# Linear attention and a GELU layer on one core: the third input of the first batch loaded in three parts, and two of its casts given to ScalarE

## The chip, the core and the metric

The kernel runs on one core of one Trainium2 chip. The metric is device time in microseconds (us) of one execution; 283.94 us is the median of three for the kernel before. Five engines of the core appear below: TensorE does the matmuls (PE in the profile, PEld for the loading of its weights), VectorE (DVE), ScalarE (ACT) and GpSimd (POOL) work on tiles, and SyncE (SP) issues most of the transfers (DMA).

## What is computed

Cut to what matters, the reference is this:

```python
batch, n_heads, seq, head_dim = (8, 8, 576, 64)        # q, k, v: float32
def phi(x): return np.where(x > 0, x, np.exp(x) - 1.0) + 1.0
q_p, k_p = (phi(q), phi(k))
kv  = np.einsum('bhsd,bhse->bhde', k_p, v)
z   = np.sum(k_p, axis=2)
num = np.einsum('bhsd,bhde->bhse', q_p, kv)
den = np.einsum('bhsd,bhd->bhs', q_p, z)[..., None] + 1e-06
x = (num / den).transpose(0, 2, 1, 3).reshape(4608, 512)
h = x @ w_in                                            # w_in 512 x 2048
g = gelu_tanh(h)
out = g @ w_out                                         # w_out 2048 x 512, out 4608 x 512 float32
```

The kernel does the matmuls in bfloat16, so every float32 input that reaches TensorE is first cast by one of the other engines. For v that is a plain cast; for q and k it happens inside phi.

## The kernel before

The eight batches are worked through in turn, the attention part of a batch being mixed into the two large matmuls of the batch ahead of it. Only batches 0 and 1 are touched by the change, and batch 0 has nothing ahead of it to hide in.

All early loads are issued at the top, on one queue, in the order in which they are needed. Heads lie in four pairs; of one pair a partition holds 576 adjacent float32 numbers (nine positions of 64).

```python
    def load_pairs(name, src, b, us=slice(0, NP)):          # NP = 4 pairs, J = 9, D = 64
        s = src[b].rearrange("h s d -> (h s d)").rearrange("(u n f) -> n u f", n=P, f=J * D)
        nc.sync.dma_start(out=ld[name, b][:, us, :], in_=s[:, us, :])
    ...
    halves = (slice(0, 2), slice(2, 4))
    for s in range(2):
        load_q_paired(0, (s,))
        load_pairs("k", k, 0, halves[s])
    for s in range(2):
        load_pairs("v", v, 0, halves[s])
    for i in range(4):
        load_w_in(i, 2 if i == 0 else 1)
    load_w_out(0)
    ...                                                     # q of batch 1, w_out(1), k of batch 1
    load_w_out(2, slice(0, 2))
    ld_tile("v", 1)
    load_pairs("v", v, 1)
    load_w_out(2, slice(2, 4))
    load_w_out(3, slice(0, 2))
    load_w_out(3, slice(2, 4))
```

The cast of v writes into a tile whose rows are 65 wide (the 65th column is the one that gives the denominator) and in which the four pairs alternate. So it reads the numbers of a partition in one run, and writes each pair as nine strips of 64 that lie 260 elements apart:

```python
    vps = [pkv.tile([P, J * NP, E], BF16, name=f"vp{i}") for i in range(2)]     # E = 65
    def cast_v_paired(b, us, fn):
        fn(
            out=vp_paired(b)[:, :, us, 0:D].rearrange("p j u d -> p u j d"),
            in_=ld["v", b][:, us].rearrange("p u (j d) -> p u j d", d=D),
        )
```

The first batch, in the order of the program (each engine takes its own instructions in this order):

```python
        keep_warm(18)                                       # matmuls on zeros
        for s in range(2):
            for n, hs in (("q", qs[s]), ("k", halves[s])):
                exp_of(n, 0, hs)                            # ScalarE
                linear_of(n, 0, hs)                         # VectorE
                least_of(n, 0, hs)                          # VectorE
        transpose_q(0, nc.scalar.copy)                      # 8 transposes, copied out by ScalarE
        keep_warm(8)
        transpose_q(1, nc.scalar.copy)
        keep_warm(5)
        for ii in range(2):
            cast_v_paired(0, halves[ii], nc.vector.tensor_copy)
        kv_ps = [bank("kv_ps", [P, E]) for _ in range(2)]
        kv_paired(0, 0, lambda a, ii: kv_ps[a])             # 36 matmuls: pairs 0 and 1
        for a, fn in enumerate((nc.vector.tensor_copy, nc.scalar.copy)):
            kv_evac(0, slice(2 * a, 2 * a + 1), kv_ps[a].rearrange("p (i e) -> p i e", i=1), fn)
        keep_warm(1)
        kv_ps = pair_of_banks("kv_ps")
        kv_paired(0, 1, lambda a, ii: kv_ps[:, a, 0:E])     # 36 matmuls: pairs 2 and 3
        kv_evac(0, slice(1, 4, 2), kv_ps[:, :, 0:E], nc.vector.tensor_copy, nc.scalar.copy)
        ...                                                 # GpSimd casts w_in and w_out
        nab_half(x[0], qt[:, 0], 0)                         # numerators and denominators
        nab_half(x[0], qt[:, 0], 1)
        ...                                                 # then x, its transposes, the first large matmul
```

Batch 1 is prepared while batch 0 is in its large matmuls: a step named `at(0, n, ...)` is issued after slot n of these. `transpose_q` and `casts` come after slot 23, `kv` after slot 27, and slot 28 is the first matmul that needs rows 10 and 11 of w_out:

```python
        def transpose_q():
            qts[b] = pt.tile([P, C, NP, P], BF16, name="qt")
            for s in range(2):
                t_ps = bank("t_ps", [P, 2, NP, P], BF16)
                ...                                         # 8 transposes
                nc.scalar.copy(qts[b][:, 2 * s : 2 * s + 2], t_ps)

        def casts():
            cast_v_paired(b, slice(0, NP), nc.vector.tensor_copy)
            cast_w_out(2, nc.vector.tensor_copy, slice(2, 4))

        def kv():
            kv_ps = [bank("kv_ps", [P, 2, E]) for _ in range(2)]
            for ii in range(2):
                kv_paired(b, ii, lambda a, ii: kv_ps[a][:, ii, :])
            ...
        at(0, 15, maps)
        at(0, 23, transpose_q)
        at(0, 23, casts)
        at(0, 27, kv)
```

Of the kernel before, what the change touches and what calls it, by code (L numbers as in the profile page):

```python
# [15 lines left out]
def kernel(  # L16
# [16 lines left out]
    nc = tc.nc  # L33
# [8 lines left out]
    NP = H // 2  # L42
# [36 lines left out]
    def bank(name, shape, dt=FP32):  # L79
        return ps_b.tile(shape, dt, name=name, tag="b")  # L80

    def pair_of_banks(name):
        return ps_a.tile([P, 2, 512], FP32, name=name, tag="a")
# [9 lines left out]
    def load_pairs(name, src, b, us=slice(0, NP)):  # L93
        s = src[b].rearrange("h s d -> (h s d)").rearrange("(u n f) -> n u f", n=P, f=J * D)
        nc.sync.dma_start(out=ld[name, b][:, us, :], in_=s[:, us, :])  # L95
# [55 lines left out]
    halves = (slice(0, 2), slice(2, 4))  # L151
    for n in "qkv":
        ld_tile(n, 0)
    for s in range(2):
        load_q_paired(0, (s,))
        load_pairs("k", k, 0, halves[s])
    for s in range(2):
        load_pairs("v", v, 0, halves[s])
    for i in range(4):
        load_w_in(i, 2 if i == 0 else 1)  # L160
    load_w_out(0)
# [29 lines left out]
    def vp_paired(b):  # L191
        return vps[b % 2].rearrange("p (j u) e -> p j u e", u=NP)
# [19 lines left out]
    def exp_of(name, b, hs=None):  # L212
        x = ld[name, b]
        hs = hs or slice(0, x.shape[1])
        if (name, b) not in exps:
            e = name + ("_e" if name != "qr" or b % 2 else "_f")
            exps[name, b] = pe.tile([P, x.shape[2] // D, x.shape[1], D], BF16, name=e)
        o, i = maps_view(name, b, x, exps[name, b], hs)
        nc.scalar.activation(o, i, AF.Exp)  # L219

    def linear_of(name, b, hs=None):
        x = ld[name, b]
        hs = hs or slice(0, x.shape[1])
        if (name, b) not in phi:
            phi_tiles(name, b)
        o, i = maps_view(name, b, x, phi[name, b], hs)
        nc.vector.tensor_scalar(o, i, 1.0, 1.0, op0=ALU.add, op1=ALU.max)  # L227

    def least_of(name, b, hs=None):
        p, e = phi[name, b], exps[name, b]  # L230
        if hs:
            p, e = p[:, :, hs, :], e[:, :, hs, :]
        nc.vector.tensor_tensor(p, p, e, op=ALU.min)  # L233
# [3 lines left out]
# [5 lines that stand above are left out]
# [169 lines left out]
    def first_batch():  # L411
        w_ps = bank("w_ps", [P, 512])

        def keep_warm(n):
            for _ in range(n):
                nc.tensor.matmul(w_ps, lhsT=warm[:, 0:P], rhs=warm)  # L416

        qt = pt.tile([P, C, NP, P], BF16, name="qt")
        qs = (slice(0, 4), slice(4, 8))

        def transpose_q(s, fn):
            t_ps = bank("t_ps", [P, C, 2, P], BF16)
            for i in range(2):
                for c in range(C):
                    h = 4 * s + 2 * i
                    nc.tensor.transpose(
                        t_ps[:, c, i, :], phi["q", 0][:, c, h : h + 2, :], ident
                    )
            fn(out=qt[:, :, 2 * s : 2 * s + 2, :], in_=t_ps)

        keep_warm(18)
        for s in range(2):
            for n, hs in (("q", qs[s]), ("k", halves[s])):
                exp_of(n, 0, hs)
                linear_of(n, 0, hs)
                least_of(n, 0, hs)
        transpose_q(0, nc.scalar.copy)
        keep_warm(8)
        transpose_q(1, nc.scalar.copy)
        keep_warm(5)  # L440
        for ii in range(2):
            cast_v_paired(0, halves[ii], nc.vector.tensor_copy)
        kv_ps = [bank("kv_ps", [P, E]) for _ in range(2)]
        kv_paired(0, 0, lambda a, ii: kv_ps[a])
        for a, fn in enumerate((nc.vector.tensor_copy, nc.scalar.copy)):
# [3 lines that stand above are left out]
        kv_paired(0, 1, lambda a, ii: kv_ps[:, a, 0:E])  # L449
        kv_evac(0, slice(1, 4, 2), kv_ps[:, :, 0:E], nc.vector.tensor_copy, nc.scalar.copy)  # L450
        for fs in (slice(0, 128), slice(128, 256), slice(256, 512)):
            cast_w_in(0, nc.gpsimd.tensor_copy, fs)
        cast_w_in(1, nc.gpsimd.tensor_copy, slice(256, 512))
        for i in range(2, 4):
            cast_w_in(i, nc.gpsimd.tensor_copy)
        for i in range(2):
            cast_w_out(i, nc.gpsimd.tensor_copy)

        xts[0] = pt.tile([P, NP, MAIN], BF16, name="xt")
        x = {0: x_tile()}  # L460

        def t(c, blocks=range(NP)):
            transpose_x(x[c], xt_chunk(0, c), nc.scalar.copy, blocks)

        def h(m, c, blocks=range(KM)):
            h_begin(0, m, slice(P * c, P * (c + 1)), blocks)

        first, second = range(2), range(2, 4)
        nab_half(x[0], qt[:, 0], 0)
        nab_half(x[0], qt[:, 0], 1)  # L470
        x[1] = nab(qt[:, 1], 0)
        t(0, first)
        h_begun[0][0] = bank("h_ps", [P, MAIN])
        nc.tensor.matmul(h_begun[0][0], lhsT=warm[:, 0:P], rhs=warm, skip_group_check=True)
        t(0, second)
        for m in range(2):
            h(m, 0, first)
        x[2] = nab_in_banks(qt[:, 2], 0)
        h(0, 0, second)
        t(1)  # L480
        h(1, 0, second)
        x[3] = nab(qt[:, 3], 0)
        cast_w_in(1, nc.vector.tensor_copy, slice(0, 256))
        h(2, 0)
        h(3, 0)
        t(2)
        for m in range(3):
            h(m, 1)
        t(3)
        gelu_table()  # L490
        h(3, 1)
        for c in (2, 3):
            for m in range(4):
                h(m, c)

    first_batch()


# [12 lines left out]
    def plan_second():  # L511
        b = 1
        x = {}

        def maps():
            for n in "qk":
                exp_of(n, b)
            cast_w_out(2, nc.scalar.copy, slice(0, 2))
            for n in "qk":
                linear_of(n, b)  # L520
            for n in "qk":
                least_of(n, b)
# [5 lines that stand above are left out]
                for c in range(2):  # L528
                    for i in range(NP):
                        nc.tensor.transpose(  # L530
                            t_ps[:, c, i, :],
                            phi["q", b][:, 2 * s + c, 2 * i : 2 * i + 2, :],
                            ident,
                        )
                nc.scalar.copy(qts[b][:, 2 * s : 2 * s + 2], t_ps)

        def casts():
            cast_v_paired(b, slice(0, NP), nc.vector.tensor_copy)
            cast_w_out(2, nc.vector.tensor_copy, slice(2, 4))

        def kv():
# [4 lines that stand above are left out]
                kv_evac(b, slice(2 * a, 2 * a + 2), kv_ps[a], fn)  # L546

        def last_w_out():
            for m, fn in enumerate((nc.gpsimd.tensor_copy, nc.scalar.copy) * 2):
                cast_w_out(3, fn, slice(m, m + 1))  # L550
            gelu_table()

        def n(c):
            x[c] = (nab_in_banks if c == 1 else nab)(qts[b][:, c], b)

        def t(c):
            if c == 0:
                xts[b] = pt.tile([P, NP, MAIN], BF16, name="xt")
            transpose_x(x[c], xt_chunk(b, c), nc.scalar.copy)
# [5 lines that stand above are left out]
        at(0, 27, last_w_out)  # L565
        at(0, 29, n, 0)
        at(0, 29, n, 1)
        at(0, 32, n, 2)
        at(0, 32, t, 0)
        at(0, 33, t, 1)  # L570
        at(0, 33, n, 3)
        at(0, 34, t, 2)
        at(0, 34.5, t, 3)
        at(0, 35, h_begin, b, 0, slice(0, 3 * P))
        at(0, 35, h_begin, b, 0, slice(3 * P, MAIN))
# [253 lines left out]
```

## Time and profile before

| what | value |
|---|---|
| time, median of three | 283.94 us (283.93 to 284.04) |
| span of the profiled execution | 282.1 us |
| TensorE busy | 276.1 us, 98% of the span |
| VectorE, ScalarE, GpSimd busy | 102.6, 164.3, 15.0 us |
| granted TensorE clock | 0.998 |
| nine casts of v on VectorE | 11.0 us in all |

The span runs from the first to the last instruction. The profile gives each engine's busy time, a picture of the span in 40 slices, the chain of work that ended last (each step followed back to what released it), and the groups of instructions with their shapes. The timeline lists one engine's instructions in order: start, length, line and operation, tiles, and in brackets how long the engine had been idle and what ended that. A count such as "x2" means that neighbouring instructions of one kind are merged, the length being that of the whole stretch. Ends of matmuls are modelled, so the start of the next one is the better mark.

### The profile page before, as it was taken

To read this page: it belongs to the slowest core of one execution; us is meant where nothing else is said; L and a number is where in the kernel's file an instruction comes from. 1 tells how busy PE (TensorE), PEld (TensorE's weight loads), DVE (VectorE), ACT (ScalarE), POOL (GpSimd) and SP (SyncE) were. 2 spreads that over 40 slices of the span, in tenths; PEclk is the share of its full clock that TensorE was granted. 3 is DMA by queue.
4 is the path that set the end of the run, shared out by engine and by line. 5 is a ranking of instruction groups with operands and counts; after the bars stand their busy time and mean duration, and the time that the engine had idled before them with its cause. 6 is when DMAs were issued, how large, how long until landed. Compare 5 with 4: busy or idle time off the path is not lost.

```text
span 282.1 us, 5465 instructions
## 1 busy us (share of the span) xinstructions
PE 276.1 (98%) x2341; PEld 135.3 (48%) x2341; DVE 102.6 (36%) x177; ACT 164.3 (58%) x224; POOL 15.0 (5%) x21
## 2 busy tenths in 40 slices
PE   8899999999999999999999999999999999999995
PEld 3474455445444544454445444544444444444444
DVE  3850386344955750356034640350124001400001
ACT  4678878786986905692569346833681364026400
POOL 3147210000000000000000000000000000000000
PEclk9999999999999999999999999999999999999999
DMA  7999999978899767916794740056405300520022
GB/s 245 401 406 397 410 402 404 404 251 222 185 379 294 263 153 212 380 26 168 188 388 114 151 131 0 2 151 168 94 2 149 114 0 2 142 81 0 2 74 74
DMA packets 59591, 53.83 MB, mean 191 GB/s; under 512 B 35760, under 2 KB 45360, under 8 KB 59568
## 3 DMA queue, kind: packets, MB, share of 16 engines
q1 hardware_dynamic: 56784, 44.58, 51.0%
q10 hardware_dynamic: 2784, 8.91, 8.7%
q8 instruction: 18, 0.29, 0.4%
q14 instruction: 5, 0.04, 0.0%
HBM read 36.70 MB, written 9.44 MB: 164 GB/s over the span
## 4 chain that ended last, share of the span: by engine, by line
PE 94%; DMA 3%; SPq 1%; DVE 1%; issue 0%; ACT 0%
PE o_ps L725 44%; PE h_ps L384 44%; DMA v_x<-in_v_dram 3%; PE n_ps L322 1%; PE n_ps L249 1%; PE kv_ps L249 1%; PE n_ps L265 1%; PE t_ps L377 1%; SPq L95 1%; SPq L100 0%; PE t_ps L530 0%; DVE vp L238 0%; DVE x L367 0%; DVE kvbd L261 0%; DVE o_sb L686 0%
## 5 line engine op out<-in xcount | busy, mean ns | idle before, releaser
L725 PE MATMUL o_ps<-w_out_sb,g 128*128 128x512 bf16 (+2 forms) x608 | 128.4, 368 | 0.0
L384 PE MATMUL h_ps<-xt,w_in_sb 128*128 128x512 bf16 (+1 forms) x564 | 113.7, 359 | 0.0
L394 ACT ACTIVATE g<-h_ps 128x512 bf16<-128x512 f32 x144 | 84.5, 599 | 36.4 <-PE h_ps L384 35.1
L384 PEld LDWEIGHTS <-w_in_sb 128*128 128x128 bf16 x628 | 58.5, 98 | 64.7
L725 PEld LDWEIGHTS <-g 128*128 128x128 bf16 x608 | 57.4, 98 | 63.5
L686 ACT COPY o_sb<-o_ps 128x512 f32<-128x512 f32 (+1 forms) x19 | 10.8, 576 | 65.7 <-PE o_ps L725 58.9
L686 DVE COPY o_sb<-o_ps 128x512 f32<-128x512 f32 (+1 forms) x19 | 12.2, 645 | 50.5 <-PE o_ps L725 45.6
L282 DVE RECIPROCAL r<-n_ps 128x6 f32<-128x6 f32 (+2 forms) x43 | 8.2, 191 | 60.9 <-PE n_ps L322 55.4
L227 DVE TENSOR_SCALAR k_p<-k_x 128x2304 bf16<-128x2304 f32 (+1 forms) x9 | 11.0, 1222 | 24.4 <-DMA k_x<-in_k_dram 24.4
L283 DVE TENSOR_TENSOR xs<-n_ps,r 128x384 bf16<-128x384 f32 (+1 forms) x30 | 17.5, 584 | 1.0
L219 ACT ACTIVATE k_e<-k_x 128x2304 bf16<-128x2304 f32 (+1 forms) x9 | 17.1, 1902 | 0.9 <-DMA k_x<-in_k_dram 0.8
L219 ACT ACTIVATE q_e<-q_x 128x2048 bf16<-128x2048 f32 (+1 forms) x9 | 15.5, 1719 | 2.8 <-DMA q_x<-in_q_dram 2.7
L227 DVE TENSOR_SCALAR q_p<-q_x 128x2048 bf16<-128x2048 f32 (+1 forms) x9 | 9.9, 1102 | 13.1 <-DMA q_x<-in_q_dram 13.1
L384 PE MATMUL h_ps<-xt_rest,w_in_sb 128*128 128x512 bf16 x64 | 14.0, 379 | 0.0
L233 DVE TENSOR_TENSOR q_p<-q_p,q_e 128x2048 bf16<-128x2048 bf16 (+1 forms) x9 | 9.9, 1100 | 6.9 <-ACT q_e L219 6.8
L407 ACT ACT_TABLE_LOAD x9 | 11.5, 1283 | 0.2
L233 DVE TENSOR_TENSOR k_p<-k_p,k_e 128x2304 bf16<-128x2304 bf16 (+1 forms) x9 | 11.0, 1221 | 1.2 <-ACT k_e L219 1.0
L238 DVE CAST vp<-v_x 128x2304 bf16<-128x2304 f32 (+1 forms) x9 | 11.0, 1223 | 0.5 <-DMA v_x<-in_v_dram 0.4
L416 PE MATMUL w_ps<-warm 128*128 128x512 bf16 x32 | 9.3, 445 | 1.2 <-DVE warm L181 1.2
L219 ACT ACT_TABLE_LOAD x8 | 10.3, 1283 | 0.1
L139 POOL CAST w_in_sb<-w_st 128x512 bf16<-128x512 f32 (+2 forms) x6 | 7.6, 1271 | 14.6 <-DMA w_st<-in_moe_w_in_dram 14.6
L283 DVE TENSOR_TENSOR x<-n_ps,r 128x512 bf16<-128x512 f32 (+1 forms) x13 | 7.9, 609 | 0.4
(50 smaller groups left out, 77.5 us busy)
## 6 DMA issues: line engine op xcount, KB each, us to landing
out_dram<-o_sb ACTq DMA_DIRECT2D x16, 512.0 KB, 3.2
k_x<-in_k_dram SPq DMA_DIRECT2D x7, 1152.0 KB, 7.2
v_x<-in_v_dram SPq DMA_DIRECT2D x7, 1152.0 KB, 11.8
q_x<-in_q_dram SPq DMA_DIRECT2D x6, 1024.0 KB, 9.6
w_st<-in_moe_w_in_dram SPq DMA_DIRECT2D x3, 1024.0 KB, 13.5
q_x<-in_q_dram SPq DMA_DIRECT2D x4, 512.0 KB, 8.5
w_st<-in_moe_w_out_dram SPq DMA_DIRECT2D x2, 1024.0 KB, 12.5
w_st<-in_moe_w_out_dram SPq DMA_DIRECT2D x4, 512.0 KB, 11.2
```

The costliest lines, as they stand in the source:

```text
L219: nc.scalar.activation(o, i, AF.Exp)
L227: nc.vector.tensor_scalar(o, i, 1.0, 1.0, op0=ALU.add, op1=ALU.max)
L233: nc.vector.tensor_tensor(p, p, e, op=ALU.min)
L238: fn(out=vp_paired(b)[:, :, us, 0:D].rearrange("p j u d -> p u j d"), in_=ld["v", b][:, us].rearrange("p u (j d) -> p u j d", d=D),)
L282: nc.vector.reciprocal(r, n_v[heads + (D,)])
L283: nc.vector.tensor_tensor(x_v, n_v[heads + (slice(0, D),)], r[heads + (None,)].to_broadcast(shape + [D]), op=ALU.mult,)
L384: nc.tensor.matmul(h_ps[:, ts], lhsT=w_in_sb[:, c, P * m : P * (m + 1)], rhs=xt[:, c, ts], start=(c == 0), stop=(c == KM - 1), skip_group_ ...
L394: nc.scalar.activation(g[:, m, :], h_ps, AF.Gelu_apprx_tanh)
L407: nc.scalar.preload_act_table_set("gelu_apprx_tanh_and_others")
L416: nc.tensor.matmul(w_ps, lhsT=warm[:, 0:P], rhs=warm)
L686: (nc.scalar.copy if on_scalar else nc.vector.tensor_copy)(dst, src)
L725: nc.tensor.matmul(o_ps, lhsT=g[:, m, P * t : P * (t + 1)], rhs=w_out_sb[:, m, fs], start=(m == 0), stop=(m == MM - 1),)
```

## The change

The first batch's v comes in three loads (pairs 0 and 1 together, then pair 2, then pair 3) in place of two. Its pair 1 is cast by ScalarE between ScalarE's two copies of the transposed q; VectorE casts pairs 0, 2 and 3, one instruction each, where it had two instructions of two pairs. In batch 1 ScalarE casts pair 3 between its two copies of q, and VectorE's one cast covers three pairs where it covered four. It is meant to have v ready for its matmuls with less of the work on VectorE, and to begin the cast of a pair as soon as that pair has come.

```diff
@@ the early loads @@
-    for s in range(2):
-        load_pairs("v", v, 0, halves[s])
+    for us in (slice(0, 2), slice(2, 3), slice(3, 4)):
+        load_pairs("v", v, 0, us)
@@ first_batch @@
         transpose_q(0, nc.scalar.copy)
         keep_warm(8)
+        cast_v_paired(0, slice(1, 2), nc.scalar.copy)
         transpose_q(1, nc.scalar.copy)
         keep_warm(5)
-        for ii in range(2):
-            cast_v_paired(0, halves[ii], nc.vector.tensor_copy)
+        for u in (0, 2, 3):
+            cast_v_paired(0, slice(u, u + 1), nc.vector.tensor_copy)
@@ plan_second, batch 1 @@
                 nc.scalar.copy(qts[b][:, 2 * s : 2 * s + 2], t_ps)
+                if s == 0:
+                    cast_v_paired(b, slice(3, 4), nc.scalar.copy)
 
         def casts():
-            cast_v_paired(b, slice(0, NP), nc.vector.tensor_copy)
+            cast_v_paired(b, slice(0, 3), nc.vector.tensor_copy)
             cast_w_out(2, nc.vector.tensor_copy, slice(2, 4))
```

## The prediction

> **What bounds the kernel now.** I read the page first: busy times, the 40 slices, then the chain.
>
> ```profile
> PE 276.1 (98%) x2341; PEld 135.3 (48%) x2341; DVE 102.6 (36%) x177; ACT 164.3 (58%) x224; POOL 15.0 (5%) x21
> PE   8899999999999999999999999999999999999995
> DMA  7999999978899767916794740056405300520022
> ```
>
> TensorE is busy 98% of the span, so a change elsewhere counts only where TensorE stands waiting. The DMA row shows the second limit: until about slice 8 (56 us) the transfers are saturated, so early data can't be hurried by any engine. The chain of waits for the first 60 us then shows the two stretches that the change touches (start, length, what):
>
> ```profile
> 3.39 8.19 DMA v_x<-in_v_dram
> 11.58 0.02 issue
> 11.60 0.77 DVE vp L238
> 12.37 0.04 issue
> 12.42 0.52 PE kv_ps L249 x31
> 12.93 0.02 issue
> 12.95 0.30 DVE kvbd L261
> ```
>
> In batch 0 the last half of v lands at 11.58 us, VectorE casts it in 0.77 us, and only then do the matmuls of pairs 2 and 3 start, at 12.42. All that follows to the first large matmuls hangs on that. The timelines of VectorE and ScalarE give the neighbours:
>
> ```profile
> 10.73 1.63 DVE L238 CAST vp<-v_x 128x1152 bf16<-128x1152 f32 x2
> 12.28 0.46 DVE L261 CAST kvbd<-kv_ps 64x65 bf16<-64x65 f32 x2
> 9.85 1.91 ACT L429 COPY qt<-t_ps 128x1024 bf16<-128x1024 bf16 x2
> 12.18 0.43 ACT L261 CAST kvbd<-kv_ps 64x65 bf16<-64x65 f32 x2 [0.41 <-PE kv_ps L249]
> ```
>
> ScalarE has a hole of 0.41 us ahead of 12.18 and VectorE none, which is why work is shifted. For batch 1 I read VectorE's timeline and the weight loads:
>
> ```profile
> 38.24 1.36 DVE L238 CAST vp<-v_x 128x2304 bf16<-128x2304 f32 x1 [0.38 <-DMA v_x<-in_v_dram]
> 39.54 0.69 DVE L145 CAST w_out_sb<-w_st 128x1024 bf16<-128x1024 f32 x1
> 39.65 0.67 PEld L249 LDWEIGHTS <-k_p 64*64 64x64 bf16 x72 [0.43 <-DVE vp L238]
> 37.83 1.89 PE L725 MATMUL o_ps<-w_out_sb,g 128*128 128x512 bf16 x8
> 40.37 1.04 PE L725 MATMUL o_ps<-w_out_sb,g 128*128 128x512 bf16 x4
> ```
>
> v lands at 38.24, its cast ends at 39.60 and the weight loads follow at 39.65. The 8 matmuls ahead pace at 1.73/8 = 0.216 us (their stretch on the chain is 1.73 us for 8), so TensorE could have gone on at 37.83 + 1.73 = 39.56: it loses only 0.1 us here now.
>
> [...]the tile's row gives 758 ns for 1152 elements and 1354 to 1365 for 2304. Their difference, 596 ns for 1152 elements, is 0.52 ns per element, with a fixed part near 158 ns. No cast of before has an odd outermost count[...].
> [...]The trace's ScalarE casts of w_out agree: 617 ns for 512, 1029 for 1024.
>
> **The change, part by part.**
>
> *The three loads.* Same bytes and same runs (576 numbers per partition and pair), one more issue of about 0.5 us on SyncE (the two of before take 1.01 us). The weight loads behind it start their issue 0.5 us later but wait more than 9 us in the queue anyhow (9.5 us from issue to landing): no cost. Halves of q and k arrive 1.4 us apart (4.49, 5.93, 7.34, 8.78 by the first uses), so v's first half is in at about 10.2, pair 2 at about 10.9, pair 3 at 11.6 as now.
>
> *ScalarE in batch 0.* 576 elements cost 617 + 64 x 0.805 = 0.67 us (slope from the two w_out casts). Behind the first q copy: 10.77 to 11.44; the second copy, 1.0 us, then ends near 12.35 in place of 11.76. Its next task, at 12.18 now, slips to about 12.3 and ends near 12.7, ahead of the first use at 12.88. Just off the path.
>
> *VectorE in batch 0.* Here I have to choose. The source of one pair is one run of 576 (even), the destination nine strips of 64 (odd). [...]**0.76 us for one pair**, as much as two pairs cost now. Three in a row, each starting about 0.09 us ahead of the end of the one before it (as neighbours on VectorE do: k_p ends at 10.82, the cast starts at 10.73): 10.73 to 11.49, 11.40 to 12.16, 12.07 to 12.83. Pairs 0 and 1 are ready at 11.49 as before. Pair 3 is ready at 12.83 in place of 12.37: the matmuls of pairs 2 and 3 start at 12.87, **0.45 us later**, although the data came no later. From 14.6 us TensorE runs without a real gap, so all is pushed by 0.45 until a wait takes it in.
>
> *Batch 1.* The source of three pairs is one run of 1728, the destination has three pairs outermost: odd, unequal. [...]**1.95 us for three pairs where four took 1.36**. From the landing at 38.24, which the saturated queue fixes, it ends at 40.19 and kv starts at 40.24 in place of 39.66: **0.58 us later**. TensorE, late by 0.45, is ready at 39.56 + 0.45 = 40.01, so the two delays don't add: the later one, 0.58, holds. The w_out cast behind it (0.69 us) goes from 40.10 to 40.79, ahead of TensorE's need at 40.95. ScalarE's extra 0.67 us lies in an idle 1.07 us before 40.58 and costs nothing.
>
> *Sum.* From kv of batch 1 on, TensorE is the bound to the end, so 0.58 us passes through: 283.94 + 0.58 = **284.52**.
>
> **Rivals.** (a) [...]pair 3 would be ready at 11.60 + 0.49 = 12.09 and the path would gain 0.28. [...]kv of batch 1 stays at 39.66, and the gain waits there for v: 283.94. For it: nothing in the trace has the slow mode.[...]
> (b) *The casts halve fully*: 0.46 us for one pair, 0.90 + 0.155 = 1.06 us for three. kv of batch 1 could start at 39.35. Then another wait takes over: the second half of w_out's third block is issued at 27.06 and takes 12.5 us, so it lands at about 39.5; its cast ends at 40.23 whatever v does, and the matmul that needs it, at 40.37 now, can move to 40.28 at most. Gain 0.09 us: 283.85.
> (c) *ScalarE becomes the bound in batch 0*: its evacuation near 12.7 would have to be 0.2 us later than reckoned to matter. This would add 0.1 to 0.2 us to (a) or (b), nothing to the main case, in which VectorE is later still.
>
> **Range and chances.** I give the slow mode 75%, (a) 15%, (b) 10%. The main case has an error of about 0.15 us either way; the others lie at 283.85 to 283.95. So I say 284.45, drawn a little down from 284.52, and 283.85 to 284.75. Two per cent would be 5.7 us; nothing here can move a tenth of that by much: within 2% at 99%.
>
> **What would show it right or wrong.** Right: casts of 128x576 on VectorE near 0.76 us, the one of 128x1728 near 1.95; kv of batch 0's second half at 12.87, kv of batch 1 at 40.24 with the weight loads waiting on VectorE; ScalarE's casts 0.67 us. Wrong: one-pair casts near 0.46 or 0.49 us, then look for the wait on v or w_out about 39 to 40.4. Also wrong if v's last pair lands later than 11.6 us, or if the push of 0.58 us is taken in by a hole in TensorE's later work that I haven't seen.

## The result, and the profile after

The changed kernel takes 284.86 us (median of six, 284.80 to 284.92) against 283.90 us before (six runs): 0.96 us slower, ratio 1.0033 with a 95% interval of 1.0020 to 1.0046. The prediction said 284.45 with a range up to 284.75. The direction and the larger part of the loss were right, and 0.1 us of the time lies outside the range.

The row of VectorE's casts of v after the change, with minimum, median and maximum in ns:

```profile
L238 DVE CAST vp<-v_x x10: 743/1353/1953, 10.7 to 163.2; 128x2304 bf16<-128x2304 f32 x6, 128x576 bf16<-128x576 f32 x3, 128x1728 bf16<-128x1728 f32 x1
```

Three pairs take 1953 ns where four took 1354 to 1365, and one pair takes 743 ns, about what two took. VectorE's timeline, and the chain of waits behind it, show what became of that in batch 0:

```profile
10.72 2.07 DVE L238 CAST vp<-v_x 128x576 bf16<-128x576 f32 x3
12.71 0.45 DVE L261 CAST kvbd<-kv_ps 64x65 bf16<-64x65 f32 x2
```

```profile
10.80 2.00 DVE vp L238 x3
12.80 0.04 issue
12.84 0.50 PE kv_ps L249 x33
```

Before, the chain came through the load of v; now it comes through VectorE, which is never idle from pair 0 to pair 3. The matmuls wait until 12.84 instead of 12.42. Two of the 36 go ahead at 12.25, because pair 2 was cast on its own, but the third already needs pair 3.

In batch 1 the chain takes a turn that the prediction didn't have:

```profile
37.51 0.46 PE t_ps L531 x8
37.97 0.02 issue
37.99 1.01 ACT qt L536
39.01 0.59 ACT vp L238
39.60 0.91 ACT qt L536
40.51 0.04 issue
40.55 0.77 PE kv_ps L249 x69
```

It runs through **ScalarE**: first copy of q, the cast of pair 3 that the change put in, second copy of q, then kv. The timelines show the order of events: first ScalarE's two copies of q before, merged into one line; then, after the change, its second copy, VectorE's cast, the weight loads of kv and the first large matmuls behind kv:

```profile
37.58 1.93 ACT L535 COPY qt<-t_ps 128x1024 bf16<-128x1024 bf16 x2 [0.37 <-PE t_ps L530]
```

```profile
39.49 1.01 ACT L536 COPY qt<-t_ps 128x1024 bf16<-128x1024 bf16 x1
38.24 1.95 DVE L238 CAST vp<-v_x 128x1728 bf16<-128x1728 f32 x1 [0.37 <-DMA v_x<-in_v_dram]
40.24 0.11 PEld L249 LDWEIGHTS <-k_p 64*64 64x64 bf16 x2 [0.60 <-DVE vp L238]
40.56 0.65 PEld L249 LDWEIGHTS <-k_p 64*64 64x64 bf16 x70 [0.21 <-issue]
41.25 1.04 PE L728 MATMUL o_ps<-w_out_sb,g 128*128 128x512 bf16 x4
```

At 40.24, the instant reckoned for VectorE's slow cast, kv does begin. It loads two weights and stops. At 40.50 ScalarE's second copy ends (before: 39.51), and at 40.56 kv goes on. The first large matmul after kv starts at 41.25, against 40.37 before: 0.88 us, of which 0.58 is VectorE's cast and 0.3 this pause. The rest comes later: on the chain of waits the changed kernel is 0.89 us behind at the next kv (63.12 against 62.23) and 0.97 behind further on (152.46 against 151.49). Where in between that is lost stays open.

Where q's copy and kv meet is in the code, not in any data. `bank()` hands out six buffers in PSUM, the memory in which the matmuls of this kernel leave their sums. When batch 1's kv asks for its two, four are held by the open sums of the output (`o_pss`), and the other two are the `t_ps` of q's transposes. So `kv_ps[0]` gets the one that the first copy frees and `kv_ps[1]` the one that the **second** copy frees; the matmuls alternate between them.

### The profile page after: what moved, and what is told of

Its sections match the earlier page's. It is cut to its first block, busy times and chain, and to the rows that moved or that the text cites. A ratio compares the mean times of both kernels' runs of the same rounds, so it can differ in the third digit from the quotient of the medians.

```text
span 283.1 us, 5467 instructions
## 1 busy us (share of the span) xinstructions
PE 277.2 (98%) x2341; PEld 135.6 (48%) x2341; DVE 103.8 (37%) x178; ACT 165.2 (58%) x226; POOL 15.0 (5%) x21
## 4 chain that ended last, share of the span: by engine, by line
PE 93%; DVE 2%; DMA 2%; ACT 1%; issue 0%; SPq 0%; DVEq 0%
PE h_ps L384 44%; PE o_ps L728 44%; DMA k_x<-in_k_dram 2%; PE n_ps L322 1%; PE n_ps L249 1%; PE kv_ps L249 1%; PE n_ps L265 1%; DVE vp L238 1%; PE t_ps L377 1%; ACT qt L536 1%; DVE k_p L233 1%; ACT k_e L219 0%; DVE q_p L233 0%; DVE k_p L227 0%; DVE q_p L227 0%
## 5 line engine op out<-in xcount | busy, mean ns | idle before, releaser
L238 DVE CAST vp<-v_x 128x2304 bf16<-128x2304 f32 (+2 forms) x10 | 12.1, 1231 | 0.4 <-DMA v_x<-in_v_dram 0.4
L416 PE MATMUL w_ps<-warm 128*128 128x512 bf16 x32 | 10.1, 471 | 1.2 <-DVE warm L181 1.2
```

Source lines behind the costliest of these rows:

```text
L238: fn(out=vp_paired(b)[:, :, us, 0:D].rearrange("p j u d -> p u j d"), in_=ld["v", b][:, us].rearrange("p u (j d) -> p u j d", d=D),)
```

## The experiments

They ran on three chips, one for each four rows of the table below, on which the kernel before takes 284.24, 284.16 and 284.14 us (283.90 in the runs of the result), and in their traces the first data come 0.1 to 0.5 us later. Beside the time I therefore use the **step past kv**: the start of the first large matmul after batch 1's kv, less VectorE's first use of q in the same trace. Before: 40.37 - 4.49 = 35.88 us. Nine of the 45 executions of kernels whose batch 0 keeps the slow casts lie about 0.8 to 1.2 us above the rest of their kernel, at a granted clock of 0.993 or 0.994 in place of 0.997 to 1.000, for a reason not tested; without them batch 0's part alone (five of 17) stands at +0.47 us, and the time of nine outermost (two of four) isn't used. Ratio and interval come from all executions and not from the two medians.

| kernel | step past kv, against 35.88 | median less before (us) | ratio, 95% interval |
|---|---|---|---|
| batch 0's part alone | +0.38 | +0.60 | 1.0028 (1.0018 to 1.0038) |
| batch 1's part alone | +0.59 | +0.44 | 1.0017 (1.0009 to 1.0024) |
| changed, kv in other banks | +0.57 | +1.21 | 1.0048 (1.0036 to 1.0060) |
| changed, halves outermost | +0.22 | +0.28 | 1.0014 (1.0007 to 1.0020) |
| changed, again | +0.85 | +0.99 | 1.0037 (1.0025 to 1.0048) |
| changed, ScalarE's cast last | +0.62 | +0.70 | 1.0025 (1.0016 to 1.0033) |
| halves outermost and cast last | -0.03 | +0.06 | 1.0000 (0.9992 to 1.0009) |
| the same, w_out's cast in two | -0.05 | +0.09 | 1.0002 (0.9993 to 1.0010) |
| changed, nine outermost | not used | +1.66, not used | 1.0048 (1.0030 to 1.0066) |
| before with three loads | +0.06 | +0.14 | 1.0003 (0.9995 to 1.0012) |
| batch 0's part alone, halves outermost | -0.26 | +0.05 | 1.0001 (0.9993 to 1.0009) |
| before, again | -0.02 | +0.04 | 1.0002 (0.9994 to 1.0010) |

**Batch 0's part alone.** Batch 1 goes back to what it was:

```diff
-                if s == 0:
-                    cast_v_paired(b, slice(3, 4), nc.scalar.copy)
-            cast_v_paired(b, slice(0, 3), nc.vector.tensor_copy)
+            cast_v_paired(b, slice(0, NP), nc.vector.tensor_copy)
```

> The three loads and batch 0's casts as in the changed kernel, batch 1 as before. Theory (batch 1's kv waits for VectorE's cast of v AND for ScalarE's second copy of q, which gives back the PSUM bank that kv writes): batch 0 costs 0.41 us, batch 1's cast of four pairs ends at 39.60 and the second copy near 39.95, so kv starts when TensorE comes, near 39.97 in place of 39.66; the time is 283.9 + 0.31 = 284.2. Rival (only VectorE's cast holds kv): the same 284.2, since TensorE itself comes last here. If it is 284.8, batch 0's part alone makes the loss, and both fall.

The step past kv moved by 0.38 rather than 0.31. VectorE's cast and then kv, from the timelines of VectorE and TensorE:

```profile
38.56 1.36 DVE L238 CAST vp<-v_x 128x2304 bf16<-128x2304 f32 x1 [0.39 <-DMA v_x<-in_v_dram]
38.56 1.89 PE L726 MATMUL o_ps<-w_out_sb,g 128*128 128x512 bf16 x8
40.38 0.78 PE L249 MATMUL kv_ps<-vp,k_p 64*64 64x65 bf16 x72
```

The eight matmuls pace out at 38.56 + 1.73 = 40.29, and kv starts 0.09 us later, though v had been ready since 39.92 and the second copy of q had ended at 40.24. That is the same gap that I took for a wait of 0.1 us in the kernel before. It is no wait for v or for a copy, so all of batch 0's delay (0.41 us between the traces of before and after) passes through. By the letter, 284.84 us is the figure at which both readings were to fall; but the kernel before takes 284.24 here, so the loss is +0.60, or the +0.47 given above the table. That is near the step; the 0.1 us between them isn't explained.

**Batch 1's part alone.** The batch 1 hunks of the change, put into the kernel before:

```diff
                 nc.scalar.copy(qts[b][:, 2 * s : 2 * s + 2], t_ps)
+                if s == 0:
+                    cast_v_paired(b, slice(3, 4), nc.scalar.copy)
-            cast_v_paired(b, slice(0, NP), nc.vector.tensor_copy)
+            cast_v_paired(b, slice(0, 3), nc.vector.tensor_copy)
```

> Batch 0 and its loads as before, only batch 1's last pair on ScalarE and three pairs on VectorE. Theory (VectorE's cast and the bank): VectorE's cast 38.24 to 40.19; ScalarE copies 37.58 to 38.55, casts to 39.2, copies to 40.1, so the bank is free before VectorE is done; kv starts at 40.24 without a pause, and the time is 283.9 + 0.58 = 284.5. Rival (batch 1's part costs about 0.9 us by itself): 284.8.

```profile
39.24 1.01 ACT L535 COPY qt<-t_ps 128x1024 bf16<-128x1024 bf16 x1
40.46 0.78 PE L249 MATMUL kv_ps<-vp,k_p 64*64 64x65 bf16 x72 [0.58 <-DVE vp L238]
```

In these lines of ScalarE's and TensorE's timelines the second copy is over at 40.25, before VectorE's cast (38.45 to 40.40), and kv runs in one piece of 0.78 us behind VectorE. The step past kv is +0.59, as the slow cast alone makes it. So the pause belongs to the **two parts together**: batch 0's delay pushes the transposes of q, and so the copies, past the end of VectorE's cast.

**kv in other banks.** Batch 1's kv is written to the pair of banks outside the pool of six:

```diff
-            kv_ps = [bank("kv_ps", [P, 2, E]) for _ in range(2)]
+            kv_ab = pair_of_banks("kv_ps")
+            kv_ps = [kv_ab[:, a, 0 : 2 * E].rearrange("p (i e) -> p i e", e=E) for a in range(2)]
```

> The changed kernel, but batch 1's kv is written into the separate pair of PSUM banks, free at that time, and so does not need a bank that ScalarE's copies of q give back. ScalarE's order is unchanged (second copy ends near 40.5). Theory (bank): the pause after two weight loads at 40.24 to 40.56 is gone, kv runs from 40.24, and about 0.32 us come back: 284.5. Rival (the pause has another cause, such as a matmul waiting for ScalarE's cast, or contention): 284.85 as in the changed kernel.

The pause went, and the time rose. ScalarE's and TensorE's timelines:

```profile
39.95 1.01 ACT L536 COPY qt<-t_ps 128x1024 bf16<-128x1024 bf16 x1
40.73 0.77 PE L249 MATMUL kv_ps<-vp,k_p 64*64 64x65 bf16 x72
42.35 0.54 ACT L261 CAST kvbd<-kv_ps 64x130 bf16<-64x130 f32 x2 [1.39 <-DVE kvbd L261]
42.94 0.63 PE L265 MATMUL n_ps<-kvbd,qt 128*128 128x130 bf16 x8 [0.47 <-ACT kvbd L261]
```

kv now runs in one piece from 40.73, **while the second copy is still under way** (to 40.96), so it needs nothing that the copy makes, and the step past kv falls to +0.57. But the two accumulators are now one tile: ScalarE's copy of the finished sums to `kvbd` (the evacuation) waits 1.39 us, until VectorE's is done, where the two started 0.02 us apart before (at 40.56 and 40.58), and TensorE then waits for it. What was won is lost twice over behind kv. The time prediction of this run was a miss; its trace answers the question.

**Halves outermost.** VectorE's odd casts get an even dimension in front, by cutting each strip of 64 into two of 32:

```diff
+    def cast_v_halves(b, us, fn):
+        fn(
+            out=vp_paired(b)[:, :, us, 0:D].rearrange("p j u (h d) -> p h u j d", h=2),
+            in_=ld["v", b][:, us].rearrange("p u (j h d) -> p h u j d", h=2, d=D // 2),
+        )
-            cast_v_paired(0, slice(u, u + 1), nc.vector.tensor_copy)
+            cast_v_halves(0, slice(u, u + 1), nc.vector.tensor_copy)
-            cast_v_paired(b, slice(0, 3), nc.vector.tensor_copy)
+            cast_v_halves(b, slice(0, 3), nc.vector.tensor_copy)
```

> The changed kernel, with the dimensions of VectorE's four odd casts of v reordered: each strip of 64 is cut into two of 32 and that dimension of 2 stands outermost on both sides; same elements, same engine. Theory ([...]bank): casts of 0.46 us for one pair and 1.06 for three in place of 0.74 and 1.95; batch 0 gains 0.28 us on the kernel before; in batch 1 ScalarE's second copy still ends near 39.85 and its bank holds kv until 39.9, so the time is 283.9 + 0.2 = 284.1. Rival (odd casts, but no bank): 283.8. Rival (the slow casts have another cause than the odd count): 284.86, casts unchanged.

The row of these casts, then lines of TensorE and VectorE from the timeline:

```profile
L244 DVE CAST vp<-v_x x4: 451/458/1060, 11.0 to 38.3; 128x576 bf16<-128x576 f32 x3, 128x1728 bf16<-128x1728 f32 x1
```

```profile
39.68 0.21 PE L255 MATMUL kv_ps<-vp,k_p 64*64 64x65 bf16 x1
40.17 0.77 PE L255 MATMUL kv_ps<-vp,k_p 64*64 64x65 bf16 x71 [0.28 <-ACT qt L542]
39.60 0.69 DVE L145 CAST w_out_sb<-w_st 128x1024 bf16<-128x1024 f32 x1 [0.23 <-DMA w_st<-in_moe_w_out_dram]
```

Same elements, same engine, other order of dimensions: 743 becomes 458 ns and 1953 becomes 1060 ns, both within 10 ns of what the casts of before give with their 0.52 ns per element and fixed part of 158 ns (0.52 x 576 + 158 = 458 and 0.52 x 1728 + 158 = 1057 ns). So the slow casts come from the order of the dimensions, not from the work or the engine. The two in front is even and also the same on both sides; nine outermost, below, tells these two apart. And with VectorE out of the way the other wait stands alone: v is cast at 39.37, TensorE is free at 37.86 + 1.73 = 39.59, **one** matmul of kv goes, the second writes to the other accumulator and waits for ScalarE's copy, which the trace now names. The third line shows the wall behind it: VectorE had to wait 0.23 us for w_out's load.

**The changed kernel again, and ScalarE's cast last.** The yardstick, and the same kernel with one word changed:

```diff
-                if s == 0:
+                if s == 1:
                     cast_v_paired(b, slice(3, 4), nc.scalar.copy)
```

> The changed kernel once more, as the yardstick beside the next three. 0.96 us above the kernel before, with batch 1's kv pausing after its first weight loads until ScalarE's second copy of q is done.

> The changed kernel, but in batch 1 ScalarE casts pair 3 after its second copy of q in place of between the two. Nothing else moves. Theory (the second copy gives back the PSUM bank that kv's second accumulator takes): the copy ends 0.6 us earlier, before VectorE's cast does, kv starts in one piece right behind VectorE's cast, and 0.3 us come back: about 0.6 us above the kernel before. Rival (kv waits for ScalarE's cast of pair 3, as data): the cast now ends where the copy ended, so nothing comes back: 0.96 above.

First kv in the yardstick's timeline, then ScalarE and TensorE in the timeline with the cast last:

```profile
40.56 0.98 PE L249 MATMUL kv_ps<-vp,k_p 64*64 64x65 bf16 x72 [0.21 <-DVE vp L238]
```

```profile
38.28 1.93 ACT L536 COPY qt<-t_ps 128x1024 bf16<-128x1024 bf16 x2 [0.58 <-PE t_ps L531]
40.09 0.70 ACT L238 CAST vp<-v_x 128x576 bf16<-128x576 f32 x1
40.60 0.78 PE L249 MATMUL kv_ps<-vp,k_p 64*64 64x65 bf16 x72 [0.18 <-DVE vp L238]
```

In the yardstick kv takes 0.98 us, with the pause in it; with the cast last the copies end at 40.21, before VectorE's cast (40.54), and kv takes 0.78 us in one piece. The cast of pair 3 ends at 40.79, when kv is already running, so it isn't that cast as data that holds kv; it is what the cast pushed back. Medians: 285.15 and 284.86, 0.29 us back, with 0.3 expected. The two intervals in the table overlap, but the step past kv falls with them, from +0.85 to +0.62. That is about batch 1's part alone (+0.59): without the pause, batch 0's delay is hidden behind VectorE's slow cast, and the two delays don't add.

**Both mended, and w_out's cast in two.** The halves and the late cast together; in the second kernel also

```diff
-            cast_w_out(2, nc.vector.tensor_copy, slice(2, 4))
+            cast_w_out(2, nc.vector.tensor_copy, slice(2, 3))
+            cast_w_out(2, nc.vector.tensor_copy, slice(3, 4))
```

> Both mended: halves of a strip outermost in VectorE's odd casts (0.46 and 1.06 us), and ScalarE's cast of pair 3 behind its second copy of q. Theory: kv starts right behind VectorE's cast, about 0.3 us ahead of the kernel before; then the matmuls on rows 10 and 11 of w_out wait for VectorE's cast of them, which cannot start before their load has landed (about 1.3 us behind v's), so only about 0.1 us is left: 0.1 us below the kernel before. If that wall were not there: 0.3 us below.

> As the run before it, and VectorE casts rows 10 and 11 of w_out in two instructions of 512 elements in place of one of 1024, so the first matmul can go after the first of them (0.43 us behind the landing in place of 0.69). Theory: the wall moves by about 0.2 us; about 0.25 us below the kernel before. If the wall is not w_out's cast, nothing changes against the run before it.

The loss is gone, but no gain shows, where 0.1 and 0.25 us were expected: ratios 1.0000 and 1.0002, with intervals that reach about 0.2 us below the kernel before. TensorE's and ScalarE's lines of the first of the two:

```profile
39.59 0.97 PE L255 MATMUL kv_ps<-vp,k_p 64*64 64x65 bf16 x72
39.34 0.70 ACT L238 CAST vp<-v_x 128x576 bf16<-128x576 f32 x1
```

kv starts 0.24 us earlier than before (34.93 against 35.17 after the first use of q), but takes 0.97 instead of 0.78 us: its second half needs pair 3, which ScalarE delivers only at 40.04. The 72 weight loads of kv take 0.86 us from 39.59 where they took 0.67 before. So the third wait is ScalarE's late cast. The first large matmul behind kv starts at 40.51, just after w_out's cast has ended (40.45). In the second kernel the first of the two w_out casts is done well before kv is, and ScalarE's late cast (to 39.97) still keeps that matmul until 40.43, so it couldn't tell whether w_out is the next wall.

**Nine outermost.** VectorE's cast of three pairs with the nine positions in front on both sides, odd but equal:

```diff
-            out=vp_paired(b)[:, :, us, 0:D].rearrange("p j u d -> p u j d"),
-            in_=ld["v", b][:, us].rearrange("p u (j d) -> p u j d", d=D),
+            out=vp_paired(b)[:, :, us, 0:D],
+            in_=ld["v", b][:, us].rearrange("p u (j d) -> p j u d", d=D),
```

> The changed kernel, VectorE's cast of three pairs in batch 1 alone reordered: the nine positions stand outermost on both sides, odd but equal. Theory[...] 1.16 us in place of 1.95. Rival (an odd outermost count is always slow): 1.95. Rival (a full halving): 1.06. The time stays near that of the changed kernel less 0.05 to 0.2 us, since ScalarE's second copy of q then holds kv.

```profile
39.32 1.15 DVE L244 CAST vp<-v_x 128x1728 bf16<-128x1728 f32 x1
```

VectorE's timeline has 1.15 us, neither 1.06 nor 1.95. It is near the 1.16 expected, but why it lies 0.09 us above the 1.06 of the halves isn't shown. So a cast with an odd count in front was fast where both sides have the same. In the slow casts (743 and 1953 ns) nine strips or three pairs stand in front at the destination alone, if the source, which lies in one run, is counted as one (no view shows how it is encoded); two and four pairs in front against such a source were fast before (758 and 1354 ns). The same trace shows the wait for the second copy once more: one matmul of kv goes at 41.59, the next at 42.09, when the copy (to 42.04) is done.

**Three loads alone; batch 0's part with halves; the kernel before again.** The first is the change's first hunk alone:

```diff
-    for s in range(2):
-        load_pairs("v", v, 0, halves[s])
+    for us in (slice(0, 2), slice(2, 3), slice(3, 4)):
+        load_pairs("v", v, 0, us)
```

The second is batch 0's part alone, as above, with

```diff
-            cast_v_paired(0, slice(u, u + 1), nc.vector.tensor_copy)
+            cast_v_halves(0, slice(u, u + 1), nc.vector.tensor_copy)
```

and the third has no edit.

> The kernel before with v's three loads alone, casts as before. Theory: no cost and no gain, since VectorE's cast of pairs 2 and 3 still waits for pair 3, which lands when it did: within 0.1 us of the kernel before. Rival (the additional load delays what is queued behind it): batch 1's v lands later and the time rises by 0.1 us or more.

> Batch 0's part alone with halves of a strip outermost, batch 1 as before. Batch 0's second kv should start about 0.2 us earlier than in the kernel before. Theory (batch 1's v is fed by the saturated loads and its cast of four pairs ends when it did): kv of batch 1 starts when it did, TensorE waits there for VectorE for about 0.2 us, and the time is that of the kernel before. Rival (the gain passes through): 0.2 us less.

> The kernel before itself, for a trace on the same chip as the experiments: how late its first loads land there, and whether its kv of batch 1 waits for VectorE. Time: the same as the kernel before.

The loads alone give 1.0003 (0.9995 to 1.0012): no effect above the uncertainty, and v of batch 1 lands 33.72 us after the first use of q, against 33.75 before. Batch 0's part with halves gave no time either (1.0001), but its trace doesn't show the reason given. It has the step past kv 0.26 us earlier, with no wait for VectorE; in that execution v of batch 1 had landed early (33.30 us after the first use) while the first data themselves had come 0.29 us later than in the repeated kernel before. Whether the gain is real and hidden in the scatter of the starts, or is taken in by v's landing in most executions, stays open: the interval reaches down to -0.2 us.

## Why the prediction was right or wrong

- **The three loads: right.** No cost (1.0003), no earlier pair 3: with the loads alone VectorE's cast of pairs 2 and 3 starts 7.18 us after the first use of q (11.91 - 4.73), against 7.11 before (11.60 - 4.49).
- **VectorE's casts of one and of three pairs slow: right**, and shown by reordering. One pair 743 ns (0.76 said), three pairs 1953 ns (1.95 said). The two figures come to twice the 0.52 ns per element of the casts of before, plus a fixed part of 155 to 158 ns; that such casts take twice as long per element was not shown by the trace of before, which has none of them. Now it is: the two differ by 1210 ns for 1152 elements, 1.05 ns each. Halves in front on both sides take 458 and 1060 ns, nine positions in front on both sides 1.15 us for three pairs.
- **Batch 0 late by 0.45: right**, 0.42 (12.84 against 12.42).
- **VectorE alone delays batch 1's kv by 0.58: right** as far as it goes. The first weights load at 40.24, as said, and batch 1's part alone gives +0.59. That it hides batch 0's delay instead of adding to it is right too, as the run with ScalarE's cast last shows (+0.62).
- **"ScalarE's extra 0.67 us lies in an idle 1.07 us before 40.58 and costs nothing": wrong, and this is the step that failed.** I looked at when ScalarE itself was next busy, not at who waits for what ScalarE finishes. The second copy of q frees the bank for kv's second accumulator. Put back by 0.41 us from batch 0 and by 0.58 from the inserted cast, it ends at 40.50, 0.31 us after VectorE's cast (40.19). That adds 0.3 to the 0.58 and makes 0.88; moving the one cast behind the copy brings 0.29 back (0.23 by the step past kv).
- **"It loses only 0.1 us here now": a misreading.** The gap of 0.1 us ahead of kv is there when v has long been ready. So the second part of the change had nothing to win where it stood.
- **Rivals.** (a) and (b) don't occur in the changed kernel. The wall of (b), w_out's late load, is seen in a trace (0.23 us of waiting), but no run shows it as the last wait. (c), ScalarE as the bound in batch 0, doesn't appear: its evacuation there starts at 12.19 as before. ScalarE became a bound in batch 1 instead, through a buffer.

## What to carry to other kernels

When work is put on an engine with idle time, follow not only that engine's next task but every buffer that its current tasks give back; count the pool at the place where the next user asks (here six banks, four held, two freed only by the copies that the new cast was put between). When a tile is divided among engines, look at what remains as an access pattern: three pairs instead of four took 1953 instead of 1354 ns, and 1060 ns with the two halves of each strip in front. And mending the faults of a change need not make it a gain: with both mended the kernel was no faster than before, because ScalarE's late cast of pair 3 then held kv.

## What was not expected of the hardware

ScalarE's cast of a pair took 0.69 us, 0.02 more than estimated, and its place between the two copies cost TensorE 0.3 us, though ScalarE still stood idle for 0.96 us ahead of its next task. TensorE's kv shows how fine the coupling is: in the run with halves outermost one matmul goes at 39.68 and the next, for another bank, 0.49 us later. The start of an execution scatters: VectorE's first use of q lies between 4.49 and 5.03 us in fourteen traces, as much as the whole effect of most of the experiments, so positions were compared after taking it off.
